# A gated activation taken as one ScalarE function, with the full value written back over its matmul's sum

## The chip, the cores and the metric

The kernel runs on one core of one Trainium2 chip. The metric is the device time of one execution in microseconds (us), the median of three runs. The engines work from instruction queues of their own: PE (TensorE) multiplies matrices, ACT (ScalarE) evaluates functions, DVE (VectorE) and POOL (GpSimd) do elementwise work, and SP issues most of the transfers. Results of matmuls land in PSUM, which ACT and DVE can read and write; everything else lies in SBUF.

## The reference

Three layers follow one another: a state-space layer over 4 sequences of 768 tokens, a dense layer with a gated activation, and eight experts of which each token uses the one with the largest logit.

```
h = x @ w_in                                  # 3072 x 256 by 256 x 2048
g = h * (1.0 / (1.0 + np.exp(-1.702 * h)))    # the gated activation
y = g @ w_out                                 # 2048 -> 256
logits = normalized(y) @ normalized(expert_emb).T / tau
probs = softmax(logits); e = argmax(logits)
out = probs[e] * (relu(y @ w1[e]) @ w2[e])
```

The matmuls run on values split in two: a rounded part ("hi") and the rest ("lo"), so that three products (hi by hi, hi by lo, lo by hi) give nearly full precision. Every factor of a matmul, the activation's value too, therefore has to be split into a hi tile and a lo tile before PE can use it.

## The kernel before, in words

The tokens lie in 8 groups (g) of 384. The dense layer's 2048 hidden units are 16 slices (f) of 128. A unit (g, f) is `gemm1`: six matmuls of 128x384 into one PSUM bank `ph`; then the activation; then `gemm2`: nine matmuls of 128x256 that add to the group's output `po`. The banks for `ph` come from a pool of two, and `gemm2` follows two units after its `gemm1`. Groups 0 and 1 run together as the first pass, and then each group has a pass of its own (g = 2 to 7).

The activation takes four instructions in before. With `xr` scaled by 0.5 later, h·(1 + tanh(0.851 h)) is twice the gated value. ACT writes `th` = tanh(0.851 ph) (line 447), DVE writes `gg` = (th + 1)·ph (line 449), which is the last reader of the bank, ACT rounds `gg` to `ghb` (line 451), and DVE takes `glb` = gg − ghb (line 453). There are four pairs of ghb and glb, used in turn.

Beside the units runs the other work. In the first pass each weight slice is decoded (`decode_w`): ACT writes `ab` and `rd` (lines 265, 267), DVE `u` twice (269, 271), POOL adds to `u` (273), DVE writes `v` (275), ACT casts it to the hi weights (276), POOL takes the lo weights (278). Slices 4 to 15 are decoded during the pass. The 24 state-space tiles (t) of the next groups pass through `ssm_a` to `ssm_d`: POOL scales `xtb` (line 293), PE, DVE and ACT work on pS, mt, pU, T, S, pY, ye, yh, and POOL writes `yl` (line 372). For the group that has just ended, `route0` copies `po` to `xr` (lines 474, 475), `dots` multiplies `xr` with the expert embeddings (line 517), and `route2` and `route3` choose the expert, the slot (`si`, line 567) and the softmax weight; POOL then scatters the tokens into a table `slots` in DRAM by three indirect transfers a group (line 132). `xr` has two buffers, so group 2's `xr` waits until group 0's scatter has landed. After the last pass the experts run in units u (lines 644 to 670); their weights are loaded late in the last pass and cast on ACT (line 598).

The order on PE, ACT, DVE and POOL is not the program's order: a scheduler simulates the engines with its own costs, and lays each engine's instructions out by it. Only SP's order is written by hand. An instruction that is longer, shorter, added or gone moves others.

Of the kernel before, what the change touches and what calls it, by code (L numbers as in the profile page):

```python
# [10 lines left out]
F32 = mybir.dt.float32  # L11
# [5 lines left out]
AF = mybir.ActivationFunctionType  # L17
ALU = mybir.AluOpType
# [4 lines left out]
D, FF, FE, NE = 256, 2048, 1024, 8  # L23
NT = NB * S
P = 128
# [5 lines left out]
TPG = 3  # L31
NG = NTILE // TPG
GT = P * TPG
# [3 lines left out]
DLEAD = 4  # L37
LOP = (0, 2)
GDOT = 6
# [87 lines left out]
def body(ctx, tc, ssm, ct, aall, cst, tok, wcat, emb, tau, w1, w2, out):  # L127
    nc = tc.nc
# [12 lines left out]
    gp = ctx.enter_context(tc.tile_pool(name="gp", bufs=2))  # L141
    rp = ctx.enter_context(tc.tile_pool(name="rp", bufs=2))
# [3 lines left out]
    slots = drp.tile([NE * ROWS, RW], F32, name="slots")  # L146
# [7 lines left out]
    def hilo():  # L154
        turn[0] += 1
        return ghb[turn[0] % NGB], glb[turn[0] % NGB]
# [8 lines left out]

# [1 line left out]
    kc = const.tile([P, K_END], F32, name="kc")  # L167
# [44 lines left out]
    loads = {"s": load_ssm, "c": load_c4, "e": load_ee, "w": load_w}  # L212
# [34 lines left out]

# [1 line left out]
    def wtile(pool, nm):  # L249
        return pool.tile([P, 2048], F32R, tag="w", name=nm)  # L250
# [3 lines left out]
    def wslice(lo, f, c0, c1):  # L254
        return dw[lo][f // 4][:, (f % 4) * 512 + c0:(f % 4) * 512 + c1]
# [23 lines left out]

# [1 line left out]
    st = {}  # L281
# [109 lines left out]

# [1 line left out]
    tokc = const.tile([P, NTILE], I32, name="tokc")  # L393
# [38 lines left out]

# [1 line left out]
    gh, gl = {}, {}  # L434
    po = {}

    def gemm1(g, f):
        pf = psh.tile([P, 512], F32, tag="h", name=f"ph{g}_{f}")
        ph = pf[:, :GT]
        n = 0  # L440
        for k in range(2):
            for w, y in ((0, yh), (0, yl), (1, yh)):
                nc.tensor.matmul(ph, lhsT=wslice(w, f, k * P, k * P + P), rhs=y[g][:, k, :], start=(n == 0),  # L443
                                 stop=(n == 5))
                n += 1
        th = gp.tile([P, GT], F32, tag="th", name=f"th{g}_{f}")
        nc.scalar.activation(out=th, in_=ph, func=AF.Tanh, scale=0.851)  # L447
        gg = gp.tile([P, GT], F32, tag="gg", name=f"gg{g}_{f}")
        nc.vector.scalar_tensor_tensor(out=gg, in0=th, scalar=1.0, in1=ph, op0=ALU.add, op1=ALU.mult)  # L449
        a, c = hilo()  # L450
        nc.scalar.copy(out=a[:, :GT], in_=gg)  # L451
        eng = nc.gpsimd if g > 1 and f % LOP[1] < LOP[0] else nc.vector
        eng.tensor_tensor(out=c[:, :GT], in0=gg, in1=a[:, :GT].bitcast(F32), op=ALU.subtract)  # L453
        gh[g, f], gl[g, f] = a, c
# [11 lines left out]

# [1 line left out]
    rt = {}  # L468
    psx = {}

    def route0(g):
        xr = rp.tile([P, TPG, RW], F32, tag="xr", name=f"xr{g}")
        for tl in (0, 1):
            nc.vector.tensor_scalar(out=xr[:, tl, :D], in0=po[g][tl], scalar1=0.5, scalar2=None, op0=ALU.mult)
        nc.scalar.mul(out=xr[:, 2, :D], in_=po[g][2], mul=0.5)
        nc.gpsimd.tensor_copy(out=xr[:, :, D:D + 1].rearrange("p t o -> p (t o)").bitcast(I32),
                              in_=tokc[:, g * TPG:(g + 1) * TPG])
        rt[g] = dict(xr=xr)
# [71 lines left out]
    def route3(g):  # L550
        xr, oh, lg, mx = (rt[g][k] for k in ("xr", "oh", "lg", "mx"))
# [5 lines left out]
        for t2 in range(TPG):  # L557
# [4 lines left out]
                                in1=base.unsqueeze(1).to_broadcast([P, TPG, NE]), op=ALU.add)  # L562
# [6 lines left out]
        ex = rp.tile([P, TPG, NE], F32, tag="ex", name=f"ex{g}")  # L569
        nc.vector.tensor_tensor(out=ex, in0=lg, in1=bc(mx), op=ALU.subtract)  # L570
        nc.scalar.activation(out=ex, in_=ex, func=AF.Exp)
        sm = rp.tile([P, TPG], F32, tag="sm", name=f"sm{g}")
# [3 lines left out]
        for tl in range(TPG):  # L576
            scatter("slots", out=slots, out_offset=bass.IndirectOffsetOnAxis(ap=si[:, tl:tl + 1], axis=0),
                    in_=xr[:, tl, :], bounds_check=NE * ROWS - 1)
        del rt[g]

# [1 line left out]
    ew = {}  # L582
# [19 lines left out]

# [1 line left out]
    EU = EARLY // P  # L604
# [192 lines left out]

# [1 line left out]
    passes = [(0, 1)] + [(g,) for g in range(2, NG)]  # L799
# [87 lines left out]
    g = NG - 1  # L887
# [48 lines left out]

# [1 line left out]
    fb = ctx.enter_context(tc.tile_pool(name="fb", bufs=1))  # L938
    with tc.For_i(0, n_over, 1) as n:
# [4 lines left out]
                                       in1=kc[:, K_PK:K_PK + 2], op0=ALU.mult, op1=ALU.add)  # L944
        w2f = fb.tile([P, NFE], F32, name="w2f")
        nc.vector.scalar_tensor_tensor(out=w2f, in0=rec[:, 2:3].to_broadcast([P, NFE]), scalar=float(FE),
                                       in1=kc[:, K_PK:K_PK + NFE], op0=ALU.mult, op1=ALU.add)
# [28 lines left out]
        for f in range(NFE):  # L976
            ph = psh.tile([P, 512], F32, tag="h", name="pho")
# [39 lines left out]
```

## Time and profile before

| | us |
|---|---|
| median of 3 runs | 629.29 (628.92 to 629.83) |
| the profiled execution's span | 630.0 |
| PE busy (share) | 563.3 (89%) |
| DVE busy | 409.7 (65%) |
| ACT busy | 260.2 (41%) |
| POOL busy | 216.2 (34%) |

The profiled execution's own time is its span, 630.0 us, 0.7 us above the median. PE is the busiest engine over the whole, but the share is a mean over stages: in the first pass other engines are full, and in the passes after it PE is. The stretches in which PE isn't full are where a change of ACT's and DVE's work can act.

### The profile page before, as it was taken

The numbers are of one execution on the slowest core, as the hardware profiler recorded it, in microseconds if no ns is written. First come the engines' busy times: TensorE is split into PE (matmuls) and PEld (weight loads), VectorE is DVE, ScalarE is ACT, GpSimd is POOL, SyncE is SP. The second block draws the span as 40 slices with busy tenths as digits, with TensorE's granted clock in tenths as the row PEclk, the third lists the DMA queues.
The fourth block names the chain that finished last, engine by engine and source line by source line (L and its number), as shares of the span: only waits on it lengthen the run. The fifth ranks groups of instructions, "written<-read, shape, count | busy, mean of one in ns | idle before, by whom it ended". The sixth has DMA issues, their size and how long they took to land.

```text
span 630.0 us, 11696 instructions
## 1 busy us (share of the span) xinstructions
PE 563.3 (89%) x4318; PEld 514.1 (82%) x4318; DVE 409.7 (65%) x1099; ACT 260.2 (41%) x577; POOL 216.2 (34%) x228
## 2 busy tenths in 40 slices
PE   5475978899999799999999999987979999999992
PEld 3253867789998699989889889976978989999992
DVE  4294799964988785875984965647675554644330
ACT  3132565543533333433434435456255533534220
POOL 4281576721114223113213112157344434524111
PEclk9589897999999899999999999998979999999996
DMA  6618549600102302102200000072155552351000
GB/s 193 155 61 205 218 132 283 162 29 1 52 2 59 82 26 79 36 26 55 61 26 26 2 1 26 8 250 71 52 168 184 182 170 75 131 163 52 24 24 24
DMA packets 32762, 56.29 MB, mean 89 GB/s; under 512 B 3306, under 2 KB 22592, under 8 KB 32576
## 3 DMA queue, kind: packets, MB, share of 16 engines
q1 hardware_dynamic: 30208, 49.22, 26.4%
q0 software_dynamic: 2496, 6.32, 2.9%
q8 instruction: 34, 0.56, 0.4%
q14 instruction: 24, 0.20, 0.1%
HBM read 44.87 MB, written 11.01 MB: 89 GB/s over the span
## 4 chain that ended last, share of the span: by engine, by line
PE 52%; issue 14%; DVE 13%; DMA 10%; POOL 5%; ACT 3%; SPq 1%; POOLq 0%; ACTq 0%; DVEq 0%
PE ph L443 19%; PE po L462 15%; DMA wer<-in_w 4%; PE qh L644 3%; PE qo L670 3%; PE po_a L462 3%; PE pS L307 3%; DVE glb L453 2%; DMA raw<-in_ssm 2%; POOL out L132 2%; PE pY L353 2%; POOL wel L600 2%; PE pY L361 2%; ACT weh L598 2%; PE pU L321 1%
## 5 line engine op out<-in xcount | busy, mean ns | idle before, releaser
L443 PE MATMUL ph<-yh,dw 128*128 128x384 f32 x512 | 162.0, 358 | 4.8 <-DVE gg L449 3.8
L443 PEld LDWEIGHTS ph<-yh,dw 128*128 128x128 f32 x512 | 96.7, 193 | 11.9 <-DVE gg L449 5.6
L447 ACT ACTIVATE th<-ph 128x384 f32<-128x384 f32 x128 | 62.4, 490 | 106.5 <-PE ph L443 105.4
L462 PE MATMUL po<-dw,ghb 128*128 128x256 f32 x576 | 102.7, 284 | 1.9 <-ACT ghb L451 1.9
L449 DVE SCALAR_TENSOR_TENSOR gg<-th,ph 128x384 f32<-128x384 f32 x128 | 70.1, 549 | 47.3 <-ACT th L447 46.2
L453 DVE TENSOR_TENSOR glb<-gg,ghb 128x384 fp32r<-128x384 f32 x128 | 82.0, 642 | 25.3 <-ACT ghb L451 24.7
L451 ACT CAST ghb<-gg 128x384 fp32r<-128x384 f32 x128 | 65.3, 512 | 63.1 <-DVE gg L449 61.7
L462 PEld LDWEIGHTS po<-dw,ghb 128*128 128x128 f32 x576 | 88.0, 188 | 3.2 <-ACT ghb L451 2.3
L443 PE MATMUL ph<-yl,dw 128*128 128x384 f32 x256 | 87.7, 343 | 0.0
L462 PE MATMUL po<-dw,glb 128*128 128x256 f32 x288 | 73.4, 294 | 0.9 <-DVE glb L453 0.7
L600 POOL TENSOR_TENSOR wel<-wer,weh 128x512 fp32r<-128x512 f32 x36 | 50.7, 1425 | 57.2 <-ACT weh L598 49.3
L293 POOL TENSOR_TENSOR xtb<-raw,einv 64x256 f32<-64x256 f32 x48 | 34.0, 708 | 105.6 <-PE pY L353 68.6
L651 DVE SCALAR_TENSOR_TENSOR glb<-qh,ghb 128x256 fp32r<-128x256 f32 (+5 forms) x72 | 35.7, 504 | 46.7 <-ACT ghb L650 45.3
L650 ACT ACTIVATE ghb<-qh 128x256 fp32r<-128x256 f32 (+5 forms) x72 | 32.2, 454 | 73.7 <-PE qh L644 72.5
L644 PE MATMUL qh<-xh,weh 128*128 128x256 f32 (+5 forms) x160 | 54.1, 338 | 8.9 <-DVE glb L651 8.1
L670 PE MATMUL qo<-weh,ghb 128*128 128x256 f32 x208 | 58.9, 292 | 1.7 <-ACT ghb L650 1.7
L517 DVE SCALAR_TENSOR_TENSOR pr<-xr,enb 128x256 f32<-128x256 f32 x144 | 60.0, 441 | 0.0
L670 PE MATMUL qo<-wel,ghb 128*128 128x256 f32 x208 | 57.6, 286 | 0.0
L462 PEld LDWEIGHTS po<-dw,glb 128*128 128x128 f32 x288 | 49.8, 189 | 4.1 <-DVE glb L453 1.7
L670 PE MATMUL qo<-weh,glb 128*128 128x256 f32 x208 | 52.9, 286 | 0.0
L644 PE MATMUL qh<-xl,weh 128*128 128x256 f32 (+5 forms) x160 | 52.0, 325 | 0.0
L644 PE MATMUL qh<-xh,wel 128*128 128x256 f32 (+5 forms) x160 | 51.9, 324 | 0.0
(176 smaller groups left out, 1074.0 us busy)
## 6 DMA issues: line engine op xcount, KB each, us to landing
wer<-in_w SPq DMA_DIRECT2D x32, 512.0 KB, 6.5
raw<-in_ssm SPq DMA_DIRECT2D x24, 384.0 KB, 7.2
wraw<-in_wcat SPq DMA_DIRECT2D x16, 512.0 KB, 9.2
slots<-padr SPq DMA_DIRECT2D x8, 516.0 KB, 10.2
ee<-ebuf SPq DMA_DIRECT2D x8, 384.0 KB
xs<-slots SPq DMA_DIRECT2D x3, 516.0 KB, 3.7
c4b<-in_ct SPq DMA_DIRECT2D x32, 48.0 KB, 4.0
xs<-slots SPq DMA_DIRECT2D x3, 387.0 KB
```

Source lines behind the costliest of these rows:

```text
L293: eng.tensor_tensor(out=xt[hs, :, :, h, :].rearrange("p c q d -> p (c q) d"), in0=r[hs, SB2 + SBT:].rearrange("p (c d) -> p c d", d=HD), i ...
L443: nc.tensor.matmul(ph, lhsT=wslice(w, f, k * P, k * P + P), rhs=y[g][:, k, :], start=(n == 0), stop=(n == 5))
L447: nc.scalar.activation(out=th, in_=ph, func=AF.Tanh, scale=0.851)
L449: nc.vector.scalar_tensor_tensor(out=gg, in0=th, scalar=1.0, in1=ph, op0=ALU.add, op1=ALU.mult)
L451: nc.scalar.copy(out=a[:, :GT], in_=gg)
L453: eng.tensor_tensor(out=c[:, :GT], in0=gg, in1=a[:, :GT].bitcast(F32), op=ALU.subtract)
L462: nc.tensor.matmul(po[g][tl], lhsT=l, rhs=r, start=(f == 0 and i == 0 and (off + tl) % 2 == 0), stop=(f == NF - 1 and i == 2), skip_group_ ...
L517: nc.vector.scalar_tensor_tensor(out=pr, in0=xr[:, tl, :D], scalar=1.0, in1=enb[:, e, :], op0=ALU.mult, op1=ALU.mult, accum_out=ld[:, tl, ...
L600: eng.tensor_tensor(out=lo[:, o], in0=r[:, i * 512:i * 512 + 512], in1=hi[:, o].bitcast(F32), op=ALU.subtract)
L644: nc.tensor.matmul(ph[:, :n], lhsT=w[:, o:o + P], rhs=x[u][:, k, :n], start=(i == 0), stop=(i == 5))
L651: nc.vector.scalar_tensor_tensor(out=c[:, :n], in0=ph[:, :n], scalar=0.0, in1=a[:, :n].bitcast(F32), op0=ALU.max, op1=ALU.subtract)
L670: nc.tensor.matmul(qacc(u, s), lhsT=l, rhs=r, start=(f == 0 and i == 0 and (s % 2 == 0 or ss is not None)), stop=(f == NFE - 1 and i == 2) ...
```

## The change

The activation becomes ScalarE's own function, x·sigmoid(1.702 x), read from `ph` twice: once written rounded to `ghb`, and once in full back over `ph`. DVE then takes `glb` = ph − ghb from PSUM and SBUF, and is now the last reader of the bank. `route0` copies without the factor 0.5. The softmax's exponential becomes (1 + t)/(1 − t) with t = tanh(x/2), which adds three small DVE instructions a group (1x24 values of each token tile). The constant that is removed selected no unit.

```diff
-        th = gp.tile([P, GT], F32, tag="th", name=f"th{g}_{f}")
-        nc.scalar.activation(out=th, in_=ph, func=AF.Tanh, scale=0.851)
-        gg = gp.tile([P, GT], F32, tag="gg", name=f"gg{g}_{f}")
-        nc.vector.scalar_tensor_tensor(out=gg, in0=th, scalar=1.0, in1=ph, op0=ALU.add, op1=ALU.mult)
         a, c = hilo()
-        nc.scalar.copy(out=a[:, :GT], in_=gg)
-        eng = nc.gpsimd if g > 1 and f % LOP[1] < LOP[0] else nc.vector
-        eng.tensor_tensor(out=c[:, :GT], in0=gg, in1=a[:, :GT].bitcast(F32), op=ALU.subtract)
+        nc.scalar.activation(out=a[:, :GT], in_=ph, func=AF.Gelu_apprx_sigmoid)
+        nc.scalar.activation(out=ph, in_=ph, func=AF.Gelu_apprx_sigmoid)
+        nc.vector.tensor_tensor(out=c[:, :GT], in0=ph, in1=a[:, :GT].bitcast(F32), op=ALU.subtract)
...
-            nc.vector.tensor_scalar(out=xr[:, tl, :D], in0=po[g][tl], scalar1=0.5, scalar2=None, op0=ALU.mult)
-        nc.scalar.mul(out=xr[:, 2, :D], in_=po[g][2], mul=0.5)
+            nc.vector.tensor_copy(out=xr[:, tl, :D], in_=po[g][tl])
+        nc.scalar.copy(out=xr[:, 2, :D], in_=po[g][2])
...
-        nc.scalar.activation(out=ex, in_=ex, func=AF.Exp)
+        nc.scalar.activation(out=ex, in_=ex, func=AF.Tanh, scale=0.5)
+        rc = rp.tile([P, TPG, NE], F32, tag="rc", name=f"rc{g}")
+        nc.vector.tensor_scalar(out=rc, in0=ex, scalar1=-1.0, scalar2=1.0, op0=ALU.mult, op1=ALU.add)
+        nc.vector.reciprocal(out=rc, in_=rc)
+        nc.vector.scalar_tensor_tensor(out=ex, in0=ex, scalar=1.0, in1=rc, op0=ALU.add, op1=ALU.mult)
```

Three places show how the scheduler lays the program out. Line numbers of the changed kernel are smaller by 1 before the activation and by 3 to 4 between it and the softmax.

The first is DVE in the middle of the first pass, where weight slices are decoded. L269 (268 after), L271 (270) and L275 (274) are the three DVE steps of a decode; in names such as gg_5_822 the number after the tile is the slice f. DVE before:

```order
98 L449 SCALAR_TENSOR_TENSOR gg_5_822<-th_5_820,ph_5_813 128x384
99 L334 TENSOR_SCALAR S_1_990<-T_0_988,dec 128x64
100 L449 SCALAR_TENSOR_TENSOR gg_4_844<-th_4_842,ph_4_835 128x384
101 L269 TENSOR_SCALAR u<-wraw_799 128x512
102 L275 SCALAR_TENSOR_TENSOR v<-ab,u 128x512
103 L339 TENSOR_TENSOR T_1_992<-pU_977,S_1_990 128x64
104 L271 SCALAR_TENSOR_TENSOR u<-wraw_799,u 128x512
105 L453 TENSOR_TENSOR glb_89<-gg_5_822,ghb_85 128x384
106 L269 TENSOR_SCALAR u<-wraw_859 128x512
107 L334 TENSOR_SCALAR S_0_1321<-T_1_992,dec 128x64
108 L453 TENSOR_TENSOR glb_90<-gg_4_844,ghb_86 128x384
```

And the same engine with the change, at the units of the same two slices:

```order
93 L449 TENSOR_TENSOR glb_89<-ph_5_786,ghb_85 128x384
94 L333 TENSOR_SCALAR S_0_1246<-T_1_947,dec 128x64
95 L274 SCALAR_TENSOR_TENSOR v<-ab,u 128x512
96 L268 TENSOR_SCALAR u<-wraw_826 128x512
97 L270 SCALAR_TENSOR_TENSOR u<-wraw_826,u 128x512
98 L449 TENSOR_TENSOR glb_90<-ph_4_805,ghb_86 128x384
99 L366 TENSOR_TENSOR ye_1072<-pY_1059,ee_528 128x256
100 L274 SCALAR_TENSOR_TENSOR v<-ab,u 128x512
101 L268 TENSOR_SCALAR u<-wraw_880 128x512
102 L270 SCALAR_TENSOR_TENSOR u<-wraw_880,u 128x512
103 L449 TENSOR_TENSOR glb_87<-ph_6_840,ghb_83 128x384
104 L274 SCALAR_TENSOR_TENSOR v<-ab,u 128x512
```

With the change one unit stands between two decodes, where two stood before: the last slice's `v` (row 129 after, row 153 before) has 18 units' `glb` ahead of it on DVE, where 21 units' `gg` and 20 units' `glb` stood before; 16 of those 20 follow the first of the pass's own decodes.

The second is POOL at the end of the pass of group 2, where the first two groups are scattered. POOL before:

```order
80 L293 TENSOR_TENSOR xtb_106<-raw_2440,einv 64x8x32 x2
81 L132 DMA slots<-xr_1563,si_1950 26624x258 x3
82 L372 TENSOR_TENSOR yl_1707<-ye_2160,yh_1706 128x2x128
83 L293 TENSOR_TENSOR xtb_105<-raw_2663,einv 64x8x32 x2
84 L476 COPY xr_2274<-tokc 128x3
85 L503 TENSOR_TENSOR rn_2324<-ss_2319,half 128x3
86 L372 TENSOR_TENSOR yl_2405<-ye_2406,yh_2404 128x2x128
87 L293 TENSOR_TENSOR xtb_106<-raw_2844,einv 64x8x32 x2
88 L132 DMA slots<-xr_1568,si_2179 26624x258 x3
```

And with the change:

```order
80 L292 TENSOR_TENSOR xtb_106<-raw_2286,einv 64x8x32 x2
81 L131 DMA slots<-xr_1461,si_1824 26624x258 x3
82 L371 TENSOR_TENSOR yl_1596<-ye_2023,yh_1595 128x2x128
83 L472 COPY xr_2132<-tokc 128x3
84 L131 DMA slots<-xr_1466,si_2042 26624x258 x3
85 L292 TENSOR_TENSOR xtb_105<-raw_2498,einv 64x8x32 x2
86 L472 COPY xr_2684<-tokc 128x3
87 L499 TENSOR_TENSOR rn_2179<-ss_2174,half 128x3
```

The `xtb` of tile 14 (the second L293 row before, the second L292 row after) followed the scatter of group 0; now it stands behind the scatter of group 1 too, and that scatter has moved ahead by four rows.

The third is DVE around the slot numbers `si` of group 1 and the copy of group 2's `xr`, which before came 26 rows before `si` of that group. DVE with the change (before has `xr` of group 2 in row 316 and `si` of groups 0 and 1 in rows 292 and 342):

```order
270 L564 TENSOR_TENSOR base<-base,pR_2027 128x8
271 L561 TENSOR_REDUCE sf_2040<-sl_2037 128x3
272 L563 CAST si_2042<-sf_2040 128x3
273 L449 TENSOR_TENSOR glb_87<-ph_15_2065,ghb_83 128x384
274 L449 TENSOR_TENSOR glb_88<-ph_0_2084,ghb_84 128x384
275 L470 COPY xr_2132<-po_0_1475 128x256 x2
276 L449 TENSOR_TENSOR glb_89<-ph_1_2111,ghb_85 128x384
```

The slot numbers of group 0 (row 243 after, at slice 11 of the pass; slice 14 before) and of group 1 (row 272) are both written before the copy of group 2's `xr` is reached.

On ACT, one load of a function table stands ahead of the first activation of the changed kernel, and none further on; before had two such loads, both in its first rows, and the changed kernel has them too.

## Rows read from the trace of the kernel before

**Rows 1.** Windows: busy us (x instructions) of each engine, PE clock, DMA share, GB/s

```profile
60.00:80.00 20.00, 15.65 (x113) 13.96 (x113) 13.46 (x21) 8.80 (x17) 9.19 (x9) 0.83 0.61 205
80.00:100.00 20.00, 16.38 (x119) 14.03 (x118) 19.82 (x29) 12.68 (x27) 14.06 (x11) 0.91 0.61 179
100.00:120.00 20.00, 16.15 (x123) 14.20 (x122) 20.00 (x31) 11.43 (x24) 12.25 (x11) 0.91 1.02 245
120.00:140.00 20.00, 19.37 (x141) 17.64 (x139) 15.09 (x25) 8.73 (x19) 9.58 (x9) 1.00 0.16 53
140.00:160.00 20.00, 20.00 (x147) 18.11 (x147) 9.33 (x20) 7.29 (x15) 1.62 (x3) 1.00 0.03 5
...
200.00:220.00 20.00, 16.21 (x146) 14.73 (x147) 14.73 (x66) 6.42 (x20) 7.52 (x11) 0.91 0.38 100
...
420.00:440.00 20.00, 14.69 (x90) 12.76 (x89) 14.40 (x21) 14.77 (x37) 15.86 (x11) 0.91 0.43 148
```

**Rows 2.** Waits in 40 to 140 us: total us, times, longest us

```profile
PE pS L307 <- issue: 6.9, 1, 6.9
...
PE po_a L462 <- DVE glb L453: 6.1, 6, 2.6
...
PE ph L443 <- DVE gg L449: 3.8, 4, 1.3
```

**Rows 3.** Groups by line and shape: busy, mean ns, idle before

```profile
L453 DVE TENSOR_TENSOR glb<-gg,ghb 128x384 fp32r<-128x384 f32 x128 | 82.0, 642 | 25.3 <-ACT ghb L451 24.7
...
L449 DVE SCALAR_TENSOR_TENSOR gg<-th,ph 128x384 f32<-128x384 f32 x128 | 70.1, 549 | 47.3 <-ACT th L447 46.2 <-issue 0.9
L451 ACT CAST ghb<-gg 128x384 fp32r<-128x384 f32 x128 | 65.3, 512 | 63.1 <-DVE gg L449 61.7 <-issue 1.2
L447 ACT ACTIVATE th<-ph 128x384 f32<-128x384 f32 x128 | 62.4, 490 | 106.5 <-PE ph L443 105.4 <-issue 0.7 <-ACT ghb L451 0.5
...
L651 DVE SCALAR_TENSOR_TENSOR glb<-qh,ghb 128x384 fp32r<-128x384 f32 x16 | 8.8, 554 | 15.1 <-ACT ghb L650 15.1
L517 DVE SCALAR_TENSOR_TENSOR pr<-xr,enb 128x256 f32<-128x256 f32 x144 | 60.0, 441 | 0.0
...
L571 ACT ACTIVATE ex<-ex 128x24 f32<-128x24 f32 x8 | 1.8, 221 | 5.0 <-DVE ex L570 5.0
```

**Rows 4.** DVE timeline 80 to 130 us: start, us, instruction

```profile
83.25 1.65 DVE L453 TENSOR_TENSOR glb<-gg,ghb 128x384 fp32r<-128x384 f32 x1
...
85.55 0.54 DVE L453 TENSOR_TENSOR glb<-gg,ghb 128x384 fp32r<-128x384 f32 x1
86.02 1.77 DVE L275 SCALAR_TENSOR_TENSOR v<-ab,u 128x512 f32<-128x512 f32 x1
...
126.94 1.10 DVE L275 SCALAR_TENSOR_TENSOR v<-ab,u 128x512 f32<-128x512 f32 x1
```

**Rows 5.** POOL timeline 80 to 100 us

```profile
83.00 1.48 POOL L278 TENSOR_TENSOR dw<-v,dw 128x512 fp32r<-128x512 f32 x1
```

**Rows 6.** Timeline 196 to 212 us, all engines

```profile
201.63 0.97 POOL L132 DMA_INDIRECT slots<-xr,si  x1 [0.30 <-issue]
...
209.32 0.76 DVE L474 TENSOR_SCALAR xr<-po 128x256 f32<-128x256 f32 x2 [4.48 <-DMA slots<-xr,si]
209.36 0.61 POOL L293 TENSOR_TENSOR xtb<-raw,einv 64x256 f32<-64x256 f32 x1 [5.19 <-DMA slots<-xr,si]
...
210.02 0.43 PE L321 MATMUL pU<-xtb,raw 128*32 128x64 f32 x16 [3.79 <-POOL xtb L293]
```

**Rows 7.** ACT timeline 404 to 447 us

```profile
415.74 1.15 ACT L598 CAST weh<-wer 128x512 fp32r<-128x512 f32 x2 [2.10 <-DMA wer<-in_w]
...
420.84 1.14 ACT L598 CAST weh<-wer 128x512 fp32r<-128x512 f32 x2 [3.16 <-DMA wer<-in_w]
```

**Rows 8.** ACT timeline 0 to 45 us

```profile
0.73 1.28 ACT L176 ACT_TABLE_LOAD   x1 [0.73 <-PEq L1007]
...
39.83 0.49 ACT L447 ACTIVATE th<-ph 128x384 f32<-128x384 f32 x1 [1.06 <-PE ph L443]
```

More of the change, by code (lines that the diff above doesn't have):

```diff
@@ L37 @@
 DLEAD = 4
-LOP = (0, 2)
 GDOT = 6
```

## The prediction

> **What bounds the kernel now.** I read the windows first. In a stretch where PE is at 20.00 of 20 us, nothing that ACT or DVE saves can be seen in the time; 140 to 160 us is such a stretch, with 147 matmuls [rows 1], and most of 140 to 400 looks like it. PE falls short in three places that the change touches. In 80 to 120 us it is busy for 16.38 and 16.15 us, while DVE is at 19.82 and 20.00: there DVE is the bound. In 200 to 220 it has 16.21, and in 420 to 440 it has 14.69 [rows 1]. So the time can fall by about 3.6 + 3.9 + 3.8 + 5.3 = 16.6 us in these windows, and by a little more through the granted clock, which is 0.91 in all of them and 1.00 in the full ones. The shortfall of 4.4 us in 60 to 80 is another matter: it belongs to one wait of 6.9 us of PE that no engine's compute ends [rows 2].
>
> Then the waits in 40 to 140 us: PE waited 6.1 us for `glb` and 3.8 for `gg`, both DVE's [rows 2]. That is 9.9 us, the most that a lighter DVE can return there.
>
> Last the groups and the DVE timeline. `glb` has a mean of 642 ns [rows 3] but two kinds: 1.65 us at 83.25, while POOL runs `dw` from 83.00 to 84.48, and 0.54 us at 85.55 [rows 4, 5]. `v` at 86.02 takes 1.77 us [rows 4]. Both have two inputs in SBUF. `gg`, of which one input lies in PSUM, has a mean of 549 [rows 3], the same as a quick `glb`. The trace thus looks like one path into SBUF that DVE's instructions with two SBUF inputs and POOL take in turns.
>
> The Trainium skill, page "SBUF — State Buffer", section "SBUF: two separate sides", says so: VectorE and GpSimd share a pair of ports, one holds it for a whole instruction, and a VectorE instruction with two SBUF inputs needs it. The 1.65 us beside 0.54 agrees. What I make of it below comes from the rows.
>
> **Part by part.**
>
> *The activation on ACT.* `th` and the cast were 490 + 512 ns a unit [rows 3]. Two functions from PSUM stand in their place, each with the input of `th`; one writes SBUF as the cast did, one writes PSUM, which no row shows. By `th` and the cast the pair costs between 0.98 and 1.02 us against 1.00: nothing. The chain is shorter, since the second no longer waits for DVE. The skill's page "ScalarE: Activation LUTs", section "Step-by-step: what each stage is for", calls ScalarE's writes to PSUM faster than those to SBUF; no row here shows such a write. By that the pair would be a little shorter, and by the rows it is the same; ACT is full in no window, so the sum doesn't change.
>
> *The table load.* One load more stands ahead of the first activation. A load took 1.28 us at 0.73, and ACT idled 1.06 us before `th` at 39.83 [rows 8]. What isn't covered is 0.22 us, and PE then still meets its wait of 6.9 us for something else [rows 2]: 0, at most +1.3 if the load begins only when `ph` is there.
>
> *DVE in the first pass.* 128 `gg` of 549 ns, 70.1 us, leave DVE [rows 3]. And `glb` gets an input in PSUM. The nearest row to the new form is line 651 of the experts, 128x384 from PSUM and SBUF, 554 ns in the mean, and it is as the quick `glb`. While slices 4 to 15 are decoded (to 126.94, the last `v` [rows 4]) 16 `glb` stand on DVE. At 0.47 us of the shared path each (85.55 to 86.02 [rows 4]) they free 16 x 0.47 = 7.5 us of it. The decodes, which take the rest of the path, end about 7.5 us sooner, at 119.5.
>
> But the new order puts less PE work ahead of that point. The last `v` has 18 `glb` ahead of it, against 21 `gg` before, so three units' matmuls move behind it. A unit is 15 matmuls, and 20.00 us held 147 of them [rows 1]: 15 x 20.00/147 = 2.04 us, three units 6.1. Once the decodes are over PE is full in both (19.37 and 20.00 in the two windows behind [rows 1]). So the pass ends 7.5 - 6.1, about 1.5 us sooner. From both sides: if all of these waits on DVE went, -9.9; if POOL, ACT and DVE still pass each decode on as slowly as now while the units are later, +3.
>
> *The end of the second pass.* The scatter of group 0 follows its `si`; its last piece was issued at 201.63, and the copy of group 2's `xr` at 209.32 and POOL's `xtb` at 209.36 waited for it to land, 4.48 and 5.19 us. PE's `pU` at 210.02 had idled 3.79 us [rows 6]. In the new order the `si` of group 0 stands at slice 11 of the pass and not at slice 14, three units or about 3 x 2.04 = 6 us sooner at least (more with state-space work between), and that of group 1 ahead of the copy. The landing then comes before the need, and the 3.79 us go. The window's clock of 0.91 [rows 1] comes back with it; the matmuls right behind the gap run slower, which I put at 0.7 us from 20 us x 0.09 = 1.8 as its most. Value 4.5, between 0 (another transfer late in its place: `xtb` now stands behind the second scatter as well) and 5.6.
>
> *The last pass.* PE's shortfall of 5.3 us in 420 to 440 goes with expert weights: ACT stood idle 2.10 and 3.16 us for loads that landed for the casts at 415.74 and 420.84 [rows 7], with the units' `ghb` casts queued behind them. The chain that leads to the loads ends in the routing of the group before, whose steps on DVE come a little sooner. The casts, though, sit among the activations on ACT, and there are now two activations that don't wait in a row. I take -1.0, from -5.3 (all of the shortfall) to +3 (about one more wait like 3.16).
>
> *The softmax and `route0`.* Three more DVE instructions a group, 24 in all, each of the size of `ex` on ACT, 221 ns [rows 3]: 24 x 0.22 = 5.3 us of DVE, beside 70.1 us that leave it. They stand behind `si` in the program, and the scatter waits for them; they are covered by the time that the scatter gains. 0, at most +0.7 for one group (3 x 0.22) where the wait at the end of the last group's routing shows. The copies in place of products cost the same.
>
> *The full passes.* From 140 on PE is full. The bank is freed by `glb` after two functions: from the start of the first, 0.49 + 0.49 + 0.55 us, against 0.49 + 0.55 before [rows 3], some 0.5 us later. With two banks and a unit of at least 2.04 us that is inside the slack: 0.
>
> **The sum** is made on the profiled execution: 630.0 - 1.5 - 4.5 - 1.0 = 623.0. That execution is 0.7 above the median of the runs, so 622.3 us.
>
> **The rivals.**
>
> *The first pass gains far more.* If the slow half of DVE's instructions goes altogether, the 9.9 us of waits go and not 1.5. For it: DVE is full to 20.00 and PE is at 16 there. Against it: the decode's own DVE steps meet POOL as before (1.77 us for `v`). 622.3 - (9.9 - 1.5) = 613.9 at the far end, about 617 in the middle.
>
> *Nothing is gained where it matters.* The decode goes DVE, POOL, DVE, ACT, POOL by turns; if its steps and not DVE's load set the pace, the first pass stays, and if the gap near 205 is handed to another transfer, so does that. Time 630.0 - 0 to 1.5, less 0.7: 628 to 629.5.
>
> *Slower: the bank comes free too late.* `glb` now both frees the bank and feeds `gemm2`, and in the passes with the dot products the order holds runs of eight of those (8 x 441 ns = 3.5 us [rows 3]) between two `glb`; before, the bank was freed by `gg`, which stood among them on its own. PE loses time once the subtraction is later than the slack, 2.04 - 0.5 = about 1.5 us. A run of eight then costs 3.5 - 1.5 = 2.0 us; with one such run in each of the six passes that have them that is 12 us, and 630.0 - 7.0 + 12 - 0.7 = 634.3. At half that price it is 628.3. Against it: PE was at 20.00 in the full passes while DVE had the same dot products and 0.55 us more a unit [rows 1, 3].
>
> *The functions don't stay loaded.* If the gated function and the softmax's needed different tables, each of 8 groups would cost two loads of 1.28 [rows 8], 8 x 2.56 = 20 us of ACT, mostly hidden, some 3 us on the path: 626. The order shows one load only, which excludes most of it.
>
> **Chances.** The forecast, 619 to 627, has 0.54; the larger gain 0.18; nothing gained 0.14; slower 0.12; the tables 0.02. What a measurement of this kernel can tell from no change is about 0.2%, 1.3 us. Of the case with nothing gained about a half is more than that below 629.3; of the late bank a sixth is within it. So faster 0.81, within 0.2% 0.08, slower 0.11. The range that holds 8 in 10 is 614 to 630.
>
> **What would show it.** Right: DVE below 20 in 80 to 120 and `glb` near 0.55 us with no 1.65 among them; the last `v` near 119.5; PE at 20.00 in 200 to 220, with the copy of `xr` waiting for no scatter; PE's matmul count the same behind 140. Wrong: `glb` still of two kinds; a PE wait for `glb` in the passes from 140 to 400, which would be the bank; or a gap at `pU` near 205 with the scatter's landing before it.

## The result, and the profile after

| | us |
|---|---|
| before | 629.56 (628.92 to 630.78, 4 runs) |
| changed | 613.57 (611.51 to 615.06, 4 runs) |
| ratio | 0.9747, 95% interval 0.9718 to 0.9777 |
| changed, in other rounds | 615.36 (613.91 to 617.71, 6 runs) |
| profiled execution's span | 609.7 |

The kernel is faster by 14 to 16 us, where 7 were forecast (622.3, range 614 to 630). The direction was right, the size was not: the first measurement lies just below the range, the one in other rounds just inside it, and the far end of the first rival was 613.9.

The profiled execution is the fastest of the four; the table's second row of the changed kernel says what is typical. The profile of before errs to the other side: wherever a span and a time are both on record, the time is 1.7 to 1.9 us longer, so the span of 630.0 stands for about 631.8, which is 2.5 us above the median and not 0.7. The forecast isn't moved by that (7.0 below the median is 622.3 either way), but the two profiles differ by 20.3 us and the medians by 16.0, so the profiles alone make the gain too large. First the windows of the changed kernel (columns as in [rows 1]):

```profile
60.00:80.00 20.00, 13.92 (x95) 11.95 (x96) 16.92 (x25) 12.65 (x25) 13.96 (x12) 0.90 0.61 218
80.00:100.00 20.00, 18.11 (x146) 16.43 (x145) 19.69 (x26) 12.79 (x27) 17.52 (x14) 0.85 0.99 279
100.00:120.00 20.00, 19.05 (x154) 17.53 (x151) 15.75 (x26) 10.50 (x23) 13.81 (x13) 1.00 0.61 156
120.00:140.00 20.00, 20.00 (x171) 18.29 (x170) 6.28 (x15) 6.26 (x15) 1.42 (x3) 1.00 0.09 27
...
180.00:200.00 20.00, 20.00 (x167) 17.90 (x166) 13.50 (x53) 8.26 (x23) 8.73 (x11) 1.00 0.34 100
200.00:220.00 20.00, 20.00 (x163) 18.46 (x162) 15.60 (x68) 7.02 (x17) 4.74 (x7) 1.00 0.03 11
...
400.00:420.00 20.00, 18.48 (x136) 17.61 (x135) 10.83 (x20) 17.50 (x43) 17.73 (x13) 1.00 0.61 209
420.00:440.00 20.00, 19.35 (x169) 18.97 (x168) 13.47 (x61) 4.88 (x14) 5.07 (x5) 1.00 0.26 86
```

Against [rows 1] all three places have moved. In 80 to 120 PE is busy for 37.2 us where it had 32.5 (but 60 to 80 has 13.92 where it had 15.65), and DVE falls from 20.00 to 15.75 in the second window. From 180 to 220 PE is full: the gap near 205 is gone. In 400 to 440 PE lacks 2.2 us, where it lacked 0.5 + 5.3 (400 to 420 had 19.48 before).

Next the groups of the activation in the changed kernel (busy, mean ns, idle before):

```profile
L449 DVE TENSOR_TENSOR glb<-ph,ghb 128x384 fp32r<-128x384 f32 x128 | 70.9, 554 | 103.5 <-ACT ph L448 100.8 <-ACT ghb L447 1.8 <-issue 0.4
...
L447 ACT ACTIVATE ghb<-ph 128x384 fp32r<-128x384 f32 x128 | 62.8, 491 | 172.5 <-PE ph L442 171.1 <-PE po L458 0.7 <-ACT yh L369 0.7
L448 ACT ACTIVATE ph<-ph 128x384 f32<-128x384 f32 x128 | 62.3, 486 | 0.0
```

The slow kind of `glb` is gone: 554 ns in the mean, where it had 642 [rows 3]. In 60 to 130 us, where the slices are decoded, the difference is plainest (min/median/max ns), before and with the change:

```profile
L453 DVE TENSOR_TENSOR glb<-gg,ghb x17: 543/965/1671, 68.6 to 128.0; 128x384 fp32r<-128x384 f32 x17
```

```profile
L449 DVE TENSOR_TENSOR glb<-ph,ghb x20: 543/548/559, 64.6 to 128.4; 128x384 fp32r<-128x384 f32 x20
```

The function written to PSUM takes 486 ns and the one written to SBUF 491; the experiments have the full value in an SBUF tile too, at 488. The Trainium skill, "ScalarE: Activation LUTs", section "Step-by-step: what each stage is for", has PSUM as the faster target; 2 to 5 ns are all that these rows show of it.

The first and the last `v` of the first pass on DVE (slices 4 and 15), in the changed kernel:

```profile
66.38 0.67 DVE L274 SCALAR_TENSOR_TENSOR v<-ab,u 128x512 f32<-128x512 f32 x1
...
111.69 0.99 DVE L274 SCALAR_TENSOR_TENSOR v<-ab,u 128x512 f32<-128x512 f32 x1
```

Before, the first of them was this, and the last is in [rows 4]:

```profile
70.27 0.68 DVE L275 SCALAR_TENSOR_TENSOR v<-ab,u 128x512 f32<-128x512 f32 x1
```

The stretch between them has gone from 56.7 to 45.3 us, and the last `v` comes 15.2 us sooner, not 7.5. DVE is full throughout the stretch in both kernels, 56.49 of 56.67 us before and 44.86 of 45.31 with the change (DVE's is the third figure behind the length):

```profile
70.27:126.94 56.67, 48.02 (x348) 42.21 (x347) 56.49 (x80) 31.67 (x63) 39.79 (x32) 0.94 0.67 182
```

```profile
66.38:111.69 45.31, 37.82 (x280) 33.77 (x281) 44.86 (x61) 27.89 (x56) 37.39 (x29) 0.89 0.81 227
```

So its length is that of DVE's instructions in it. These are the activation's before (71 to 126.9 us), and then with the change (67.2 to 111.6; busy us, mean ns):

```profile
L453 DVE TENSOR_TENSOR glb<-gg,ghb 128x384 fp32r<-128x384 f32 x15 | 15.6, 1044 | 0.0
...
L449 DVE SCALAR_TENSOR_TENSOR gg<-th,ph 128x384 f32<-128x384 f32 x15 | 8.1, 542 | 0.2 <-ACT th L447 0.2
```

```profile
L449 DVE TENSOR_TENSOR glb<-ph,ghb 128x384 fp32r<-128x384 f32 x12 | 6.5, 545 | 0.0
```

`gg` took 8.1 us and `glb` has 9.1 less, a part of it because three units fewer stand in the stretch. Against that the decode's own `u` and `v` take 33.8 us where they took 29.1; closer together as they are, they seem to meet POOL more often.

The matmuls that end the first pass (min/median/max ns, first and last start), of the kernel before and of the changed one:

```profile
L462 PE MATMUL po_a<-dw,glb x96: 278/282/582, 48.1 to 160.1; 128*128 128x256 f32 x96
```

```profile
L458 PE MATMUL po_a<-dw,glb x96: 278/281/422, 45.9 to 151.5; 128*128 128x256 f32 x96
```

The last one starts at 151.5 us, where it started at 160.1.

The whole span, stage by stage in us, gives what each part was worth. A pass ends where the last matmul of its `gemm2` starts. "Three others" are runs of the experiments that keep the old activation with `gg` in SBUF (the softmax alone, and the two with three `xr` buffers); "again" is the changed kernel in other rounds.

| stage | before | three others | changed | again | forecast |
|---|---|---|---|---|---|
| start to first `v` | 70.3 | 67.0 to 67.4 | 66.4 | 68.2 | 0 |
| first to last `v` | 56.7 | 55.7 to 56.6 | 45.3 | 46.4 | -7.5 |
| last `v` to the end of the first pass | 33.2 | 33.2 | 39.8 | 39.9 | +6.1 |
| pass of group 2 | 44.1 | 44.1 to 45.1 | 44.2 | 44.2 | 0 |
| pass of group 3 (the gap near 205) | 51.5 | 52.1 to 53.2 | 46.1 | 46.1 | -4.5 |
| passes of groups 4 to 6 | 134.7 | 136.4 to 138.7 | 135.7 | 135.7 | 0 |
| pass of group 7 and the experts | 239.6 | 236.9 to 237.6 | 232.2 | 233.6 | -1.0 |

Up to the first `v` the change gained nothing: it is the profile of before that started late, and 3.9 of the 15.2 us lie there. From the first `v` on, the first pass gained 2.6 to 4.7 us, the pass of group 3 gained 5.4 to 7.1, and the last pass with the experts 3.3 to 7.5. For groups 4 to 6 the executions disagree (-1.1 to 2.9).

At the end of group 2's pass POOL now has its wait for group 0's scatter in the copy of the token column (POOL timeline):

```profile
182.43 1.22 POOL L131 DMA_INDIRECT slots<-xr,si  x1 [1.32 <-issue]
...
192.71 0.19 POOL L472 COPY xr<-tokc 128x3 int32<-128x3 int32 x1 [5.70 <-DMA slots<-xr,si]
```

POOL still waits 5.70 us, but PE doesn't need what stands behind it so soon. The extra table load stands where it was forecast (ACT timeline):

```profile
37.42 1.28 ACT L447 ACT_TABLE_LOAD   x1
38.71 0.49 ACT L447 ACTIVATE ghb<-ph 128x384 fp32r<-128x384 f32 x1
```

And the late bank, the rival on the slow side: this is all that PE waited in 120 to 400 us of the changed kernel (total us, times, longest):

```profile
PE ph L442 <- DVE glb L449: 1.5, 2, 1.2
```

In 40 to 140 us, the first pass, it is PE's longest wait, where the bank cost 3.8 us before [rows 2]:

```profile
PE ph L442 <- DVE glb L449: 5.4, 4, 1.9
...
PE po_a L458 <- ACT ghb L447: 0.6, 1, 0.6
```

So the activation's waits there went from 9.9 us [rows 2] to 6.0, and to 7.3 in the other rounds (6.7 + 0.6): those of `gemm2` for `glb` are gone, and those for the bank have grown.

### The profile page after: what moved, and what is told of

Its sections match the earlier page's. It is cut to its first block, busy times and chain, and to the rows that moved or that the text cites. A ratio compares the mean times of both kernels' runs of the same rounds, so it can differ in the third digit from the quotient of the medians.

```text
span 609.7 us, 11558 instructions
## 1 busy us (share of the span) xinstructions
PE 555.5 (91%) x4318; PEld 511.7 (84%) x4318; DVE 349.7 (57%) x995; ACT 249.5 (41%) x578; POOL 213.8 (35%) x228
## 4 chain that ended last, share of the span: by engine, by line
PE 56%; DMA 13%; issue 12%; DVE 8%; POOL 4%; ACT 2%; SPq 2%; POOLq 0%; ACTq 0%; DVEq 0%
PE ph L442 20%; PE po L458 15%; DMA wer<-in_w 4%; PE qh L645 4%; PE qo L671 4%; PE po_a L458 3%; DMA wraw<-in_wcat 3%; PE pS L306 3%; PE pY L352 2%; POOL out L131 2%; DMA raw<-in_ssm 2%; POOL wel L601 2%; PE pY L360 2%; PE pU L320 2%; DMA slots<-padr 2%
## 5 line engine op out<-in xcount | busy, mean ns | idle before, releaser
L442 PE MATMUL ph<-yh,dw 128*128 128x384 f32 x512 | 163.8, 361 | 9.0 <-DVE glb L449 7.0
L447 ACT ACTIVATE ghb<-ph 128x384 fp32r<-128x384 f32 x128 | 62.8, 491 | 172.5 <-PE ph L442 171.1
L449 DVE TENSOR_TENSOR glb<-ph,ghb 128x384 fp32r<-128x384 f32 x128 | 70.9, 554 | 103.5 <-ACT ph L448 100.8
L442 PEld LDWEIGHTS ph<-yh,dw 128*128 128x128 f32 x512 | 95.2, 190 | 18.2 <-DVE glb L449 9.5
L458 PE MATMUL po<-dw,ghb 128*128 128x256 f32 x576 | 104.1, 287 | 0.1
L458 PEld LDWEIGHTS po<-dw,ghb 128*128 128x128 f32 x576 | 84.0, 189 | 1.6 <-ACT ghb L447 0.3
L601 POOL TENSOR_TENSOR wel<-wer,weh 128x512 fp32r<-128x512 f32 x36 | 49.5, 1391 | 57.0 <-ACT weh L599 56.6
L458 PE MATMUL po<-dw,glb 128*128 128x256 f32 x288 | 68.4, 282 | 0.5 <-DVE glb L449 0.5
L292 POOL TENSOR_TENSOR xtb<-raw,einv 64x256 f32<-64x256 f32 x48 | 33.1, 689 | 100.1 <-PE pY L352 72.7
L448 ACT ACTIVATE ph<-ph 128x384 f32<-128x384 f32 x128 | 62.3, 486 | 0.0
L645 PE MATMUL qh<-xl,weh 128*128 128x256 f32 (+5 forms) x160 | 51.8, 323 | 0.0
L645 PE MATMUL qh<-xh,wel 128*128 128x256 f32 (+5 forms) x160 | 51.8, 323 | 0.0
L131 POOL DMA_INDIRECT out<-ob,xs x29 | 30.6, 1057 | 52.7 <-DVE ob L682 47.7
```

Source lines behind the costliest of these rows:

```text
L131: i = nc.gpsimd.indirect_dma_start(in_offset=None, oob_is_err=False, **kw)
L292: eng.tensor_tensor(out=xt[hs, :, :, h, :].rearrange("p c q d -> p (c q) d"), in0=r[hs, SB2 + SBT:].rearrange("p (c d) -> p c d", d=HD), i ...
L447: nc.scalar.activation(out=a[:, :GT], in_=ph, func=AF.Gelu_apprx_sigmoid)
L448: nc.scalar.activation(out=ph, in_=ph, func=AF.Gelu_apprx_sigmoid)
L449: nc.vector.tensor_tensor(out=c[:, :GT], in0=ph, in1=a[:, :GT].bitcast(F32), op=ALU.subtract)
L458: nc.tensor.matmul(po[g][tl], lhsT=l, rhs=r, start=(f == 0 and i == 0 and (off + tl) % 2 == 0), stop=(f == NF - 1 and i == 2), skip_group_ ...
```

## The experiments

Theory A: while the weights are decoded DVE itself is full, so both the `gg` that left and the time that `glb` stood waiting for POOL count. Theory B: only the shared path counts. The first eight runs look at the first pass, the tables, the scatter; the last four at the turn to the experts, the gap near 205 and the best version.

### The softmax's part alone

```diff
-        nc.scalar.activation(out=ex, in_=ex, func=AF.Exp)
+        nc.scalar.activation(out=ex, in_=ex, func=AF.Tanh, scale=0.5)
+        # then rc = 1 - ex, rc = 1 / rc, ex = (ex + 1) * rc on DVE
```

> The kernel before with the softmax's exponential taken through tanh, nothing else. Both theories of the first pass (A: what counts is DVE's own full time there, of gg and of the time that glb waits for POOL; B: what counts is the path into SBUF alone) leave this part out: 629.6 within 1.3 us, its 24 small DVE instructions hidden. A rival, that part of the gain comes from this edit's reshuffling, gives 626 or less.

Measured 632.64 (ratio 1.0057, interval 1.0035 to 1.008): slower by about 3 us, where 1.3 at most was expected; where they are lost wasn't found. None of the gain comes from this edit by itself. Its profiled execution was the fastest of ten (span 628.8), and its window of 200 to 220 us still holds the gap (PE has 16.94 of 20).

### The activation alone, with Exp kept

```diff
-        nc.scalar.activation(out=ex, in_=ex, func=AF.Tanh, scale=0.5)
-        # and the three DVE instructions behind it
+        nc.scalar.activation(out=ex, in_=ex, func=AF.Exp)
```

> The changed kernel with the softmax's Exp kept: the order then has a table load before and after nearly every group's softmax, 15 more than the changed kernel. If the loads are hidden behind PE (ACT is 41 percent busy): 613.6 within 1.5 us. If each pair of loads (2 x 1.28 us) holds up an activation on which the next unit waits, about 1 us a group: 621.

Measured 620.37. The table loads in its groups:

```profile
L447 ACT ACT_TABLE_LOAD x8 | 10.3, 1283 | 1.1 <-PE ph L442 0.8
L568 ACT ACT_TABLE_LOAD x8 | 10.3, 1283 | 0.1
```

Sixteen loads of 1.283 us where the changed kernel has one: 19 us more of ACT. The kernel is 5 to 7 us slower with them, near the second of the two expectations; how much of that is the loads, and how much the order that goes with them, the run doesn't tell. So the softmax through tanh, which costs 3 us alone, keeps 5 to 7 with the new function. "ScalarE: Activation LUTs" of the Trainium skill, section "What ACT_TABLE_LOAD costs", gives about 1283 ns for a load; the rows agree.

### The full value in SBUF, everywhere and in the first pass alone

```diff
-        nc.scalar.activation(out=ph, in_=ph, func=AF.Gelu_apprx_sigmoid)
-        nc.vector.tensor_tensor(out=c[:, :GT], in0=ph, ...)
+        gg = gp.tile([P, GT], F32, tag="gg", name=f"gg{g}_{f}")   # everywhere; or: ph if g > 1 else this
+        nc.scalar.activation(out=gg, in_=ph, func=AF.Gelu_apprx_sigmoid)
+        nc.vector.tensor_tensor(out=c[:, :GT], in0=gg, ...)
```

> The changed kernel with the second function written to an SBUF tile and not back into PSUM: glb has two SBUF inputs again and can wait for POOL, and the bank is free one step earlier. DVE's order around the last decode is the same as in the changed kernel (18 glb ahead of the last v). Theory A (both the gg that left and the waiting of glb count, about half each): the last v of the first pass some 7 us later than 111.7, total 618 to 621. Theory B (only the shared path counts): the last v near 125, total 623 to 625. A rival, that the path costs nothing and only gg's leaving counts: 613.6, last v near 112.

> The mirror of the run with PSUM in the first pass: the full value goes to an SBUF tile in the first pass and over its sum in PSUM from group 2 on. DVE has no gg, but glb has two SBUF inputs while the slices are decoded. If POOL's share of the path makes that pass's time: its end is as before, near 160, against 152 with the change, and the total is 621 to 624. If only DVE's lost gg counts: 614 to 616.

Measured 617.8 everywhere, and 620.4 in the first pass alone. Everywhere, the last `v` came at 121.2, between A's 119 and B's 125; in the first pass alone, that pass ended at 159.3, as one of the two expectations had it. DVE's first and last `v` in the run with SBUF in the first pass alone, and its `glb` between 60 and 130 us (min/median/max ns):

```profile
70.10 0.67 DVE L274 SCALAR_TENSOR_TENSOR v<-ab,u 128x512 f32<-128x512 f32 x1
...
121.75 0.68 DVE L274 SCALAR_TENSOR_TENSOR v<-ab,u 128x512 f32<-128x512 f32 x1
```

```profile
L450 DVE TENSOR_TENSOR glb<-gg,ghb x18: 543/558/1646, 66.9 to 129.4; 128x384 fp32r<-128x384 f32 x18
```

`glb` is of two kinds again, up to 1.65 us, and the decodes take 51.7 us: 6.4 more than with PSUM, 5.0 less than before. That agrees with A; B would have all 11.4 back. The same twelve `glb` as with the change stand in that stretch, and they make up the 6.4 us by themselves (12.9 against 6.5, here in 70.9 to 121.7 us):

```profile
L450 DVE TENSOR_TENSOR glb<-gg,ghb 128x384 fp32r<-128x384 f32 x12 | 12.9, 1076 | 0.0
```

In the time, the first pass alone in SBUF costs 5.0 to 6.8 us (620.4 against 615.4 and 613.6). From the first `v` to the end of the pass it has 89.2 us, as before (88.9 to 89.9) and not as with the change (85.1 and 86.3): without the quick `glb`, `gg`'s leaving didn't shorten the pass at all.

### DVE's load given back

```diff
+        if g < 2:
+            ex = gp.tile([P, GT], F32, tag="gg", name=f"gg{g}_{f}")
+            nc.vector.scalar_tensor_tensor(out=ex, in0=a[:, :GT].bitcast(F32), scalar=1.0, in1=ph,
+                                           op0=ALU.add, op1=ALU.mult)
         nc.vector.tensor_tensor(out=c[:, :GT], in0=ph, ...)
```

> The changed kernel with one more DVE instruction of gg's kind (SBUF and PSUM in, 128x384 out, read by nobody) ahead of each glb of the first pass. It gives DVE the time of gg back and lets glb's input stay in PSUM. If DVE's own full time counts in the first pass: most of that pass's gain of 8 to 10 us goes, 620 to 623. If only the waiting for the shared path counts: 613.6 to 615.5.

Measured 621.45. Its first and last `v`, and its `glb` between 60 and 130 us:

```profile
71.56 0.68 DVE L274 SCALAR_TENSOR_TENSOR v<-ab,u 128x512 f32<-128x512 f32 x1
...
123.35 1.74 DVE L274 SCALAR_TENSOR_TENSOR v<-ab,u 128x512 f32<-128x512 f32 x1
```

```profile
L452 DVE TENSOR_TENSOR glb<-ph,ghb x17: 542/545/560, 71.0 to 129.8; 128x384 fp32r<-128x384 f32 x17
```

Here `glb` is always quick, and the decodes still take 51.8 us, 6.5 more than with the change. Not all of that is DVE's own work. Just ahead of the last `v` DVE stood idle for PE, and PE for a load of the state-space part:

```profile
120.66 2.04 PE L306 MATMUL pS<-c4b,raw 128*128 128x256 f32 x4 [3.33 <-DMA raw<-in_ssm]
```

```profile
122.74 0.69 DVE L309 TENSOR_TENSOR mt<-pS,kc 128x512 f32<-128x512 f32 x1 [3.62 <-PE pS L306]
```

That leaves about 2.9 us of the 6.5, in the slowest of the four executions. The time speaks against B more clearly: all four, from 617.2 to 624.8 us, lie above its 613.6 to 615.5. Whether the load was late by chance or by the order isn't shown. The bank, which the extra instruction holds longer, isn't the reason: PE waited 4.3 us for it in 40 to 140 us, less than with the change.

### gg kept on DVE, but in PSUM

```diff
-        gg = gp.tile([P, GT], F32, tag="gg", name=f"gg{g}_{f}")
+        gg = ph
```

> The kernel before with gg written back over its sum in PSUM, from where ACT rounds it and DVE subtracts: gg stays on DVE, but glb no longer has two SBUF inputs. The order has si of group 1 ahead of group 2's xr, so the gap near 205 should be gone (about 4.5 us) in every theory. Theory A: half of the first pass's gain besides, last v near 120, total 619 to 622. Theory B: all of it, last v near 113, total 613 to 617. If only gg counts: last v near 126, total 625.

Measured 630.91: a miss in every theory. The last `v`, and PE's wait for the bank in 40 to 140 us:

```profile
117.87 0.79 DVE L275 SCALAR_TENSOR_TENSOR v<-ab,u 128x512 f32<-128x512 f32 x1
```

```profile
PE ph L443 <- DVE glb L453: 6.6, 4, 2.5
```

The decodes behaved as A says (49.2 us, the last `v` at 117.9). But this order puts only 16 `glb` ahead of the last `v`, where 18 stand with the change and 20 stood before. More of PE's work is left behind it, 43.0 us against 39.8 and 33.2, and the pass ends at 160.9. The bank is now held through four instructions, `th`, `gg`, the cast and `glb`, on two engines by turns, but PE's 6.6 us for it are no more than the 5.4 and 6.7 of the changed kernel, so they don't tell the two apart. The gap near 205 stayed too (PE waited 5.4 us for `xtb`), though `si` of both groups stood ahead of group 2's `xr`: that place in the order isn't enough to remove it. Why the pass of group 2 took 56.4 us here, against 44.1, wasn't followed up.

### Three buffers for xr, and then xtb off POOL

```diff
+        xr = rp.tile([P, TPG, RW], F32, tag="xr", name=f"xr{g}", bufs=3)   # th: bufs=3, gg = th
...
+            eng = nc.vector if t == 14 or t in XV[h] else nc.gpsimd          # the second run only
```

> The kernel before with three buffers for xr in place of two (and gg written over th, which gives the room), so that group 2's xr needn't wait for group 0's scatter. If that wait made the gap near 205 us: the gap goes, and the time falls by 4 to 5 us, to about 625.5. If the scatter's landing holds POOL's xtb for another reason, the gap stays: 629.9.

> The kernel before with three xr buffers, and with tile 14's xtb taken by DVE and not by POOL. POOL's next instruction that waits for group 0's scatter to land is then one that PE needs only much later. If the gap near 205 us is PE waiting for an xtb that stands behind that wait on POOL: the gap of 4 to 5 us goes, 625 to 626. If the transfers themselves are late (the landing of the state-space load as well): no change, 629.9.

Measured 629.94 and 632.95: the gap stays in both (PE has 15.51 and 15.42 us of 20 in 200 to 220). In the first PE waits as before, 4.5 us, for POOL's `xtb`. In the second it is another wait, of the same length and in the same place:

```profile
PE pS L307 <- DMA raw<-in_ssm: 4.6, 1, 4.6
```

So two waits lie on each other: `xtb` behind the scatter's landing, and `pS` behind the landing of the next state-space tile, which is in flight with the scatter. Taking one away uncovers the other. In the kernel before that load was issued here and took 8.8 to 9.3 us to land, that is until about 210.5, and its `pS` ran at 210.63:

```profile
201.47 9.41 SPq L203 DMA_DIRECT2D raw<-in_ssm  x3
```

With the change the same load is issued at 185.11 and its `pS` runs at 202.79, 17.7 us later and not 9.2. That the second run is 3.4 us slower than before isn't explained.

### The two forms by pass

```diff
-        gg = gp.tile([P, GT], F32, tag="gg", name=f"gg{g}_{f}")
+        gg = ph if g < 2 else gp.tile(...)                     # PSUM in the first pass
+        gg = ph if g < 2 or g == NG - 1 else gp.tile(...)      # and in the last
```

> The changed kernel with the full value written over its sum in PSUM in the first pass only, and to an SBUF tile from group 2 on, as the run with the SBUF tile did everywhere. That run gained 6 to 7 us in the passes of groups 2 to 6 over the changed kernel's own. If that comes from the bank that is free one step earlier and the order that follows: about 607 to 609. If it was chance of that one order: 613.6.

> The changed kernel as it is, to have it on the same chip and in the same rounds as the others: 613.6 within 2 us.

> The run with PSUM in the first pass and SBUF from group 2 on, once more, beside the changed kernel: if its gain holds, 3 to 4 us under the changed kernel, about 610; if it was the chip of that time, the same as the changed kernel.

> The full value goes over its sum in PSUM in the first pass and in the last one (group 7), and to an SBUF tile in between. In the last pass POOL makes the experts' lo weights from SBUF, and with the SBUF tile glb took up to 1.7 us there, against 0.56 with PSUM. If the changed kernel's 6 us in the turn from the dense layer to the experts come from that: 5 to 6 us under the run with PSUM in the first pass alone, about 604 to 605. If they come from loads that happened to land sooner: the same as that run, about 610.

Measured: PSUM in the first pass 610.1, and 607.2 in the rounds in which the changed kernel had 615.36 (8.2 less, where 3 to 4 were expected); PSUM in the first and the last pass 602.81 (601.32 to 604.27; ratio to before 0.9567, interval 0.9535 to 0.96). That last version beats both kernels. It does as the run before it up to the end of group 6's pass (367.4 us in both profiles), and the last pass with the experts decides: 235.1 us against 240.2. `glb` in 396 to 436 us, PSUM in the first pass alone:

```profile
L450 DVE TENSOR_TENSOR glb<-gg,ghb x4: 1129/1629/1721, 398.1 to 409.2; 128x384 fp32r<-128x384 f32 x4
```

and PSUM in the first and the last pass:

```profile
L450 DVE TENSOR_TENSOR glb<-ph,ghb x4: 544/552/558, 399.6 to 407.0; 128x384 fp32r<-128x384 f32 x4
```

In the turn POOL makes the experts' lo weights from SBUF, and `glb` meets it there as it meets the decodes in the first pass. PE's wait for it in 385 to 430 us, in the one and in the other:

```profile
PE po L459 <- DVE glb L450: 3.3, 3, 2.9
```

```profile
PE po L459 <- DVE glb L450: 0.5, 1, 0.5
```

These 2.8 us are the larger part of the difference; the order of the last pass differs too, and the rest may be its doing.

In the passes between, where POOL has little to do, the SBUF form is the quicker one: groups 2 to 6 take 212.0 us in the run of 607.2, where the changed kernel took 226.1, although PE counts as all but full in either (the last pass with the experts then takes 241.2 against 233.6). The busy time of 220 to 400 us, first of the changed kernel and then with SBUF everywhere:

```profile
220.00:400.00 180.00, 180.00 (x1449) 165.70 (x1449) 97.73 (x377) 67.40 (x173) 37.24 (x49) 1.00 0.12 37
```

```profile
220.00:400.00 180.00, 180.00 (x1545) 169.05 (x1538) 104.03 (x408) 71.03 (x178) 41.29 (x52) 1.00 0.12 38
```

PE is at 180.00 of 180 in both, with 1449 matmuls in the one and 1545 in the other (not all of one size). With the SBUF form the bank is free one function earlier, and PE's state-space work of these passes stands in longer runs (the same 564 matmuls in 56 pieces and not in 76). Which of the two counts was not tried apart.

## Why the prediction was wrong

The parts that it named are the parts that moved, but three terms of its sum were too small, two of them by much.

*The first pass: -1.5 forecast, -2.6 to -4.7 measured.* The step that failed is the size of DVE's relief: "At 0.47 us of the shared path each they free 16 x 0.47 = 7.5 us of it. The decodes ... end about 7.5 us sooner, at 119.5." It priced the shared path alone and put the `gg` that leave at nothing. But DVE itself was full, so the stretch was as long as its instructions, and 8.1 us of `gg` left as well as 9.1 of `glb`, of which the decode's own steps took 4.7 back. The stretch fell by 9.3 to 11.4 us. That the last `v` came 15 us sooner, twice the 7.5, is in part chance: 3.9 of them lie ahead of the first `v`, where the profile of before was late. The term that was taken off held: 6.6 us more PE work behind the last `v`, where 6.1 was forecast.

*The last pass: -1.0 forecast, -3.3 to -7.5 measured.* This is the largest miss, and its cause is open. The prediction looked at ACT's casts and not at POOL. The last run shows that the contention of the first pass stands there too, and that the new activation written to SBUF costs 4.4 us in that pass (607.2 against 602.8). But it doesn't show that this is what the change gained over before: there `glb` took up to 1.29 us in the turn, and PE waited only 0.7 us for it, against 0.5 with the change.

*The gap near 205: -4.5 forecast, -5.4 to -7.1 measured.* The 3.8 us of the wait and the clock came back (PE is full from 180 to 220 at 1.00). The cause is half right. The prediction had the scatter alone; the runs with three `xr` buffers show a second wait beneath it. With the change group 0's scatter starts 30.9 us after the end of the first pass, where it was 38.6, and the load too has more time before it is needed. No run moved the scatter alone, so that its place in the order removed the gap is argued, not shown.

The time that was measured is the one that the first rival names at its far end, 613.9, but that is luck. It let all 9.9 us of PE's waits in the first pass go; 2.6 to 3.9 of them went, and the rest of the gain came from the other two places.

The rule at the start of the prediction, that nothing which ACT or DVE saves can be seen where PE is at 20.00 of 20, failed as well. The SBUF form from group 2 on took 14 us out of passes in which PE was all but full either way.

The table load, the cost on ACT and the bank in the full passes came out as forecast: one load, 0.49 us for each function, and 1.5 us of waits for the bank in 280 us. The slow rival is refuted there. Its mechanism is at work in the first pass, where the prediction gave it no price: the bank is freed later, and PE's wait for it grew from 3.8 us to 5.4 and 6.7. The rival of the tables was too cheap: 5 to 7 us where the tables do alternate, not 3.

Some of its small sums are a little off, without effect: 7.5 - 6.1 is 1.4, half way to 613.9 is 618, and the shares as stated give 0.09 within 0.2% and 0.10 slower.

## What to carry to other kernels

When an engine is full to 20.00 of 20 in the stretch that matters, the stretch is as long as its instructions: add up those that leave and those that get shorter, and ask which of the others will now collide more. Here both `gg` and the slow `glb` had to go; with the slow `glb` back, the first pass was as long as before. Look for the same contention in every stretch where the two engines meet, not only in the one where it is most visible. A gap can be held by two waits of one length: before crediting a change with it, see what would end next. And compare more than two profiles before taking a difference for the change's: here one of them started 3 us late.

## What the runs showed of the hardware

A DVE instruction of 128x384 with both inputs in SBUF took 0.53 to 1.72 us, the long ones beside POOL; with one input in PSUM it took 0.52 to 0.56 in every run, whatever POOL did. ACT writing 128x384 to PSUM, over its own input, took 484 to 487 ns, against 488 to an SBUF tile of the same type and 491 to the rounded one.
